# Turning and storing the last quarter of the output by TensorE, in a fused attention and feed-forward kernel

## The chip, the core and the metric

The kernel runs on one core of a Trainium2 chip. The metric is the device time of one execution in microseconds (us). The kernel before took 904.01 us, the median of three runs (902.47 to 904.57). A separate execution was recorded by the hardware profiler; all profile times below are from it, counted from the start of its span. In the profile PE is TensorE (matmuls; PEld its weight loads), DVE is VectorE, ACT is ScalarE, POOL is GpSimd and SP is SyncE, which only issues transfers. A "q" after a name (SPq, ACTq) means the engine's instruction queue.

## The reference

Attention with a mask by cluster: every query and key is assigned to the nearest of 16 centroids of its head, and a query sees only keys of its own cluster. Its output, laid out as 3072 tokens by 512 features, goes through two matrix products with a gate between them. All is float32.

```python
mask = q_assign[:, :, :, None] == k_assign[:, :, None, :]
scores = np.where(mask, scale * np.matmul(q, k.transpose(0, 1, 3, 2)), -1e9)
attn = softmax(scores)                              # over the keys
x = np.matmul(attn, v).transpose(0, 2, 1, 3).reshape(B * S, H * D)   # 4*768, 8*64
h = x @ w_in                                        # 512 -> 2048
g = h * (1.0 / (1.0 + np.exp(-1.702 * h)))
return (g @ w_out).astype(np.float32)               # 2048 -> 512, the output
```

The inputs arrive as 64-bit floats. The kernel reads them as pairs of 32-bit words and makes float32 weights of them itself, which it calls rounding.

## The kernel before, in words

The kernel has a fast path, `fast`, and behind it a `general` one. `fast` returns a number `bad`; a branch at L34 jumps over `general` when it is 0, as it is here. Every engine takes this branch when it has come to the end of its own part of `fast`.

`fast` has two stages. In the first, until about 343 us, attention is computed for 16 pairs of heads in 96 steps of a hand-written order (L665 to L708). In two of the six steps of a pair, `step()` is called five times; each call lets `rounding()` issue its next VectorE instruction. A piece of weights is 128 partitions by 512 columns; pieces 0 to 15 are `w_in`, pieces 16 to 31 are `w_out`. A piece takes five VectorE instructions, and the last of them, at L207, adds two parts and writes the float32 weights. For `w_out` it writes the columns in another order: column 128*r + 32*n + t of the matrix goes to place 128*n + 32*r + t.

In the second stage the tokens of one batch entry (768) pass through both products before those of the next. Each product is done by a scheme with seven multiplications in place of eight for a matrix cut into two by two, and the second product (`second49`) cuts each of the seven once more. The output of a batch entry is gathered in four tiles, `Y[11]`, `Y[12]`, `Y[21]` and `Y[22]`: the first digit is the half of the output columns, the second the half of the tokens. Each has the output columns on the partitions (128 by 2, the second called `m`) and 384 tokens on the free axis. In the last call of `second49` (k = 6, i = 4) the sums that complete `Y[21]` are made by VectorE at L928, L929 and L933. The last one adds the last product to the tokens of `q` = 0 (192 tokens, the first half of the tile) with `m` = 1.

Because the tiles have columns on the partitions, they are turned before they are stored. `store` does it with VectorE's transpose, which turns blocks of 32 by 32 each in its place (L957). After it, a partition holds, for a token, 32 columns of `m` = 0 and 32 of `m` = 1; with the order of `w_out`'s columns these are 64 neighbouring columns of the output, 256 bytes. Four transfers, one for each group of 32 partitions, store a tile or a part of it (L961). The tiles `E` and `T_of` hold the turned data.

For the last batch entry, `Y[22]` is turned and stored within the last call of `second49`. Within it too, before the last product (`extra(2)`, the generator `tail`), `q` = 1 of `Y[21]` is turned and stored by four transfers on SP, and `m` = 0 of `q` = 0 is turned. After the call, `m` = 1 of `q` = 0 is turned, and `q` = 0 is stored by four transfers, alternately on SP and on ScalarE's queue (L1066).

The order of the instructions on an engine is that of the program text, and each engine waits by counters for what it needs from another. Each transfer, too, counts up one of eight counters when it has landed. The counters are given out by the framework, not in the text.

Of the kernel before, what the change touches and what calls it, by code (L numbers as in the profile page):

```python
# [8 lines left out]
FP32 = mybir.dt.float32  # L9
# [5 lines left out]
ALU = mybir.AluOpType  # L15
# [23 lines left out]
def fast(  # L39
# [26 lines left out]
    nc = tc.nc  # L66

    B, H, S, D = q.shape
    NC = centroids.shape[1]
    DM, DF = moe_w_in.shape  # L70
    P = 128
# [12 lines left out]
    SQ = 32  # L84
# [10 lines left out]
        name="spill", bufs=1, space=bass.MemoryType.DRAM))  # L95
# [13 lines left out]
        name="dram", bufs=2, space=bass.MemoryType.DRAM))  # L109
# [3 lines left out]
    def bank():  # L113
        return ps_m.tile([P, 512], FP32, name="m")
# [42 lines left out]
    WN = 512  # L157
# [6 lines left out]
    NW = len(w_chunks)  # L164
    w_raw, w_pow = {}, {}

    def load_w(i):
        if i < NW:
            t = wp.tile([P, WN, 2], I32, name="raw")
            nc.sync.dma_start(out=t.rearrange("p n t -> p (n t)"),  # L170
                              in_=w_chunks[i][1])
            w_raw[i] = t
# [7 lines left out]
    def rounding():  # L180


        i = w_done[0]
        load_w(i + 2)
        raw, w = w_raw.pop(i), w_chunks[i][0]
        e = wp.tile([P, WN], I32, name="e", bufs=2)
        a = bank()
        hi, lo, a_i = raw[:, :, 1], raw.bitcast(U32)[:, :, 0], a.bitcast(I32)
        nc.vector.tensor_scalar(out=a_i, in0=hi, scalar1=3, scalar2=0x3FFFFFF8,
                                op0=ALU.logical_shift_left,  # L190
                                op1=ALU.bitwise_and)
        yield
        nc.vector.scalar_tensor_tensor(out=a_i, in0=hi, scalar=ODD, in1=a_i,
                                       op0=ALU.bitwise_and, op1=ALU.bitwise_or)
        yield
        nc.vector.tensor_scalar(out=e, in0=a_i, scalar1=POWER, scalar2=None,
                                op0=ALU.bitwise_and)
        yield
        e = e.bitcast(FP32)
        nc.vector.scalar_tensor_tensor(out=e, in0=lo, scalar=2.0 ** -52, in1=e,  # L200
                                       op0=ALU.mult, op1=ALU.mult)
        yield
        if i >= NW // 2:
            w, a, e = (w.rearrange("p (n r t) -> p r n t", r=P // SQ, t=SQ),
                       *(x.rearrange("p (r n t) -> p r n t", r=P // SQ, t=SQ)
                         for x in (a, e)))
        nc.vector.tensor_tensor(out=w, in0=a, in1=e, op=ALU.add)  # L207

        check_w(i, raw, raw.bitcast(FP32)[:, :, 1])
        w_done[0] += 1  # L210
        yield
# [13 lines left out]
    def check_w(i, raw, z):  # L225

        tests.append(lambda: nc.scalar.activation(  # L230
            out=z, in_=raw.bitcast(FP32)[:, :, 1], func=AF.Square,
            accum_out=row_sums[:, 2, i:i + 1]))
        tests.append(lambda: nc.scalar.activation(
            out=z, in_=z, func=AF.Exp, scale=-2.0 ** 12,
            bias=fifteen[:, 0:1], accum_out=row_sums[:, 3, i:i + 1]))
# [7 lines left out]
    ident = const.tile([P, P], FP32, name="ident")  # L243
# [46 lines left out]
    def keep_busy(n):  # L290
        for _ in range(n):
# [8 lines left out]
                        identity=ident)  # L300
    for a in range(2):
        rows = slice(a * D, (a + 1) * D)
        nc.vector.tensor_copy(
            out=cT[rows, :, a, :],
            in_=cps[rows, 0:P].rearrange("d (h a c) -> d h a c", a=2,
                                         c=NC)[:, :, a, :])
# [290 lines left out]
    T_of = {}  # L597
# [44 lines left out]
    for p in range(1, NPAIR):  # L642
        for i in range(2 if p == 1 else 0, len(PREP)):
            t = 2 * TG * (p - 1) + (0, 0, 0, 0, 1, 2, 2)[i]
# [65 lines left out]
    while tests:  # L710
# [14 lines left out]
    QT = HALF // 2  # L725
# [4 lines left out]
    ps_b = ctx.enter_context(tc.tile_pool(name="ps_b", bufs=6, space=PS))  # L730
    G = sp.tile([P, NF, 2, HALF], FP32, name="G")
    Z_of = {i: sp.tile([P, FB, DN], FP32, name=f"Z{i}") for i in (1, 2, 4)}
    Y = {n: acc_p.tile([P, 2, HALF], FP32, name=f"Y{n}")
         for n in (11, 12, 21, 22)}
# [31 lines left out]
    def turn_w(i):  # L766
        a = W_of(i)
        sums(nc.vector, ((a(0, 1), a(0, 0), "-", a(0, 1)),))
# [110 lines left out]
    def after7(f):  # L879

        sums(nc.vector, ((G[:, f, 1], G[:, f + FB, 1], "-", G[:, f, 1]),))
        if f >= FQ:
            for _ in sums_t(0, slice(f - FQ, f - FQ + 1)):
                pass

    def second49(k, extra, last):
# [45 lines left out]
        if i == 4:  # L932
# [9 lines left out]
                    5: ((Y[12], y, "+", Y[12]), (Y[22], y, "+", Y[21])),  # L942
                    7: ((Y[22], y, "+", Y[22]), (Y[21], y, "+", Y[21]))}[i])

    def store(b, n, m=slice(0, 2), q=slice(0, 2), queues=(nc.sync,),
              turned=slice(0, 2)):

        h, t = divmod(n, 10)
        h, t = h - 1, t - 1
        o = {11: T_of[4], 12: E[0], 22: E[1], 21: E[2]} if b < B - 1 else {  # L950
            11: T_of[4], 12: T_of[4], 22: T_of[2], 21: T_of[3]}
        o = o[n].rearrange("p a t -> p (a t)").rearrange(
            "p (j m i) -> p j m i", m=2, i=SQ)
        at, to = q.start * QT, q.stop * QT
        o = o[:, at // SQ:to // SQ]
        for one in range(turned.start, turned.stop):
            nc.vector.transpose(out=o[:, :, one], in_=Y[n][:, one, at:to])  # L957
        rows = out[b * S + t * HALF + at:b * S + t * HALF + to]
        for r in range(P // SQ if queues else 0):
            col = r * P + (2 * h + m.start) * SQ  # L960
            queues[r % len(queues)].dma_start(  # L961
                out=rows[:, col:col + (m.stop - m.start) * SQ].rearrange(
                    "(j t) i -> t j i", t=SQ),
                in_=o[r * SQ:(r + 1) * SQ, :, m].rearrange(
                    "t j m i -> t j (m i)"))
# [20 lines left out]
    def do(steps, n):  # L986
        for _ in range(n):
            next(steps, None)
# [3 lines left out]
    for b in range(B):  # L992
        for f in range(FB):
            first7(b, f, *XT)
            sums_w(b * FB + f + 2)
            if f:
                after7(f - 1)
            do(pend, 1)
            if b == 0 and f < 3:
                for n in range(3 * f, min(3 * f + 3, FB)):  # L1000
                    sums_z((nc.gpsimd, nc.vector, nc.vector)[n % 3], n)
            if b == 0 and f in (3, 4):
                for i in ORDER[0:4] if f == 3 else ORDER[4:]:
                    turn_w(i)
            if b == 0 and f >= 3:
                for k in {3: (0,), 4: (1, 2), 5: (3,), 6: (4,), 7: ()}[f]:
                    keep_w(k, spare_y())
                if 5 <= f < 7:
                    load_sums(f - 5)
        after7(FB - 1)  # L1010
        if b < B - 1:
            for h in range(2):
                for hp in range(HP):
                    x = xT_of[b + 1, h, hp] = xp.tile([P, HALF], FP32,
                                                      name="x")
                    nc.sync.dma_start(out=x, in_=kept[b, h, hp])
            made = sums_x(b + 1)
        else:
            made = iter(())

        def stores(b, *todo, **how):
            for n in todo:
                store(b, n, **how)
                yield

        def tail():
            store(b, 22)
            yield
            store(b, 21, q=slice(1, 2))
            store(b, 21, q=slice(0, 1), queues=(), turned=slice(0, 1))  # L1030
            yield

        def chain(*todo):
            for steps in todo:
                yield from steps

        def sums_of_x():
            for XT[:] in made:
                yield

        x_steps = sums_of_x()
        final = b == B - 1

        for k in range(7):
            nxt = sums_t(k + 1) if k < 6 else iter(())
            more = {1: sums_G(6), 2: sums_G(5), 3: sums_G(4),
                    4: stores(b, 11), 5: stores(b, 12) if final else x_steps,
                    6: tail() if final else x_steps}.get(k, iter(()))
            if b == B - 1 and k < 2:
                test(k)  # L1050
            if (b, k) == (B - 1, 6):
                is_bad = nc.values_load(bad[0:1, 0:1], min_val=0, max_val=1)

            def extra(at):
                do(nxt, (2, 1, 1)[at])
                do(more, ((1, 0, 1) if final else (0, 4, 4))[at] if k == 6
                   else (0, 0, 4)[at] if k == 2 else (0, 2, 2)[at])

            second49(k, extra, final)
            if k < 5:  # L1060
                load_sums(k + 2, b == 0 and k > 2)
            elif b < B - 1:
                load_sums(k - 5)
        pend = () if final else stores(b, 12, 22, 21)
        if final:
            store(b, 21, q=slice(0, 1), turned=slice(1, 2),  # L1066
                  queues=(nc.sync, nc.scalar))
    return is_bad
@with_exitstack
def general(  # L1070
# [436 lines left out]
```

## Time and profile before

| | |
|---|---|
| median of three runs | 904.01 us |
| the profiled execution's own time | 905.66 us |
| its span in the profile | 903.8 us |
| TensorE busy | 885.9 us |
| VectorE busy | 728.1 us |
| end of the last matmul | 892.2 us |
| mean granted TensorE clock | 0.995 |

The span is from the first to the last instruction of the program. The profiled execution's own time is 1.9 us longer than its span. A row of the profile names line, engine, operation, what is written and read, shapes and count. The timeline gives start, duration, engine and line, and joins neighbours of one kind. The list of waits says which instruction waited for which, for how long in total, how often, and the longest.

### The profile page before, as it was taken

How to read it: one execution, taken by the hardware profiler on the slowest of the kernel's cores; microseconds unless marked ns; L12 is line 12 of the kernel's file. 1: busy time of each engine (PE TensorE's matmuls, PEld its weight loads, DVE VectorE, ACT ScalarE, POOL GpSimd, SP SyncE). 2: the span in 40 equal slices, each digit the busy share in tenths (PEclk: the TensorE clock that was granted, in tenths of full speed). 3: DMA queues.
4: the chain of work that ended last, by engine and by line, in shares of the span. 5: the costliest groups of instructions: out<-in, count | busy, mean ns of one | idle time of the engine just before them, and what ended most of it. 6: DMA issues, size and time to landing. Idle time of an engine off the chain costs nothing.

```text
span 903.8 us, 17747 instructions
## 1 busy us (share of the span) xinstructions
PE 885.9 (98%) x6712; PEld 581.7 (64%) x6712; DVE 728.1 (81%) x1170; ACT 365.0 (40%) x816; POOL 499.2 (55%) x469
## 2 busy tenths in 40 slices
PE   8999999999999999999999999999999999999994
PEld 3444444444454445558996557997557997557994
DVE  3999989999898997998998557797556797556894
ACT  3677767776777764222111222112222112222110
POOL 5899999999999998693274211242221242220230
PEclk9999999999999999999999999999999999999998
DMA  9466556666664210036213102332102322200323
GB/s 181 113 123 116 103 119 134 139 140 137 138 134 112 85 43 18 9 127 214 70 54 122 36 1 71 105 86 83 42 1 70 106 74 90 47 1 1 105 73 71
DMA packets 177565, 78.97 MB, mean 87 GB/s; under 512 B 154440, under 2 KB 160704, under 8 KB 177472
## 3 DMA queue, kind: packets, MB, share of 16 engines
q1 hardware_dynamic: 176912, 77.63, 35.3%
q8 instruction: 55, 0.90, 0.4%
q14 instruction: 38, 0.31, 0.1%
q10 hardware_dynamic: 560, 0.13, 0.1%
HBM read 61.03 MB, written 16.70 MB: 86 GB/s over the span
## 4 chain that ended last, share of the span: by engine, by line
PE 88%; DVE 6%; issue 2%; POOL 2%; DMA 1%; SPq 0%; ACT 0%; DVEq 0%; POOLq 0%
PE b L850 32%; PE b L900 23%; PE s L468 13%; PE o L533 12%; PE m L550 3%; PE s L491 3%; DVE G L594 2%; POOL sum L517 2%; DVE E L594 1%; PE m L344 1%; DVE Tx L594 1%; DMA in<-in_k_dram 1%; DVE y L841 0%; PE o L292 0%; DMA Wz<-kept_w 0%
## 5 line engine op out<-in xcount | busy, mean ns | idle before, releaser
L517 POOL TENSOR_TENSOR sum<-sum,A 128x384 f32<-128x384 f32 x252 | 265.9, 1091 | 26.7 <-ACT A L499 16.0
L841 DVE TENSOR_TENSOR G<-b,G 128x384 f32<-128x384 f32 x224 | 123.2, 557 | 98.9 <-PE b L850 89.3
L499 ACT ACTIVATE A<-s 128x768 f32<-128x768 f32 x192 | 146.2, 808 | 91.8 <-PE s L491 73.0
L594 POOL TENSOR_TENSOR Y<-y,Y 128x768 f32<-128x768 f32 x28 | 69.2, 2487 | 174.9 <-DVE y L841 151.0
L855 ACT ACTIVATE G<-G 128x384 f32<-128x384 f32 x128 | 66.4, 523 | 199.0 <-DVE G L841 197.7
L468 PE MATMUL s<-T,T 64*64 64x384 f32 x1536 | 143.0, 487 | 0.7 <-ACT A L499 0.7
L533 PE MATMUL o<-A,inv 64*64 64x384 f32 x1536 | 141.4, 483 | 0.0
L594 POOL TENSOR_TENSOR W<-w_in 128x256 f32<-128x256 f32 x32 | 23.6, 738 | 163.8 <-PE b L850 163.5
L594 DVE TENSOR_TENSOR G<-G 128x768 f32<-128x768 f32 (+1 forms) x92 | 102.3, 1136 | 0.0
L468 PEld LDWEIGHTS s<-T,T 64*64 64x64 f32 x1536 | 55.2, 132 | 69.9 <-ACT A L499 36.4
L850 PE MATMUL b<-Tx,w_in 128*128 128x384 f32 x256 | 93.0, 486 | 0.0
L850 PE MATMUL b<-x,W 128*128 128x384 f32 x256 | 93.0, 486 | 0.0
L850 PE MATMUL b<-x,w_in 128*128 128x384 f32 x256 | 88.6, 486 | 0.0
L533 PEld LDWEIGHTS o<-A,inv 64*64 64x64 f32 x1536 | 59.1, 133 | 37.9 <-issue 32.8
L850 PEld LDWEIGHTS b<-x,W 128*128 128x128 f32 x256 | 48.6, 190 | 33.9
L850 PEld LDWEIGHTS b<-Tx,w_in 128*128 128x128 f32 x256 | 48.6, 190 | 33.9
L850 PEld LDWEIGHTS b<-x,w_in 128*128 128x128 f32 x256 | 48.5, 190 | 33.5 <-issue 0.6
L900 PE MATMUL b<-G,w_out 128*128 128x192 f32 x320 | 55.9, 326 | 0.0
L900 PEld LDWEIGHTS b<-G,w_out 128*128 128x128 f32 x320 | 52.7, 190 | 1.1
L900 PE MATMUL b<-E,Wz 128*128 128x192 f32 x288 | 51.5, 328 | 1.4 <-DVE E L594 1.4
L900 PEld LDWEIGHTS b<-E,Wz 128*128 128x128 f32 x288 | 47.1, 190 | 3.4 <-POOL Wz L594 1.3
L850 PE MATMUL b<-Tx,W 128*128 128x384 f32 x128 | 46.6, 487 | 1.5 <-DVE Tx L594 1.5
(165 smaller groups left out, 1366.9 us busy)
## 6 DMA issues: line engine op xcount, KB each, us to landing
Wz<-kept_w SPq DMA_DIRECT2D x78, 256.0 KB
raw<-in_moe_w_in_dram SPq DMA_DIRECT2D x16, 512.0 KB
raw<-in_moe_w_out_dram SPq DMA_DIRECT2D x16, 512.0 KB
inv<-in_v_dram SPq DMA_DIRECT2D x16, 384.0 KB
in<-in_q_dram SPq DMA_DIRECT2D x60, 96.0 KB
in<-in_k_dram SPq DMA_DIRECT2D x60, 96.0 KB
kept<-x SPq DMA_DIRECT2D x24, 192.0 KB
x<-kept SPq DMA_DIRECT2D x24, 192.0 KB
```

The source lines that it names most:

```text
L344: nc.tensor.matmul(out=ps[r:r + SQ, w * NJ * SQ:(w + 1) * NJ * SQ] .rearrange("p (j t) -> p j t", t=SQ), lhsT=cT[:, p % HP].rearrange("p a ...
L468: nc.tensor.matmul(out=ps[c:c + D, a, 0:HALF], lhsT=T[p, 1][rows, kt * P + c:kt * P + c + D], rhs=T[p, 0][rows, h * HALF:(h + 1) * HALF], ...
L491: nc.tensor.matmul(out=s_of[u][c:c + D, a, :], lhsT=rows_of[1, p % 2][rows, kt * P + c:kt * P + c + D], rhs=rows_of[0, p % 2][rows, h * HA ...
L499: nc.scalar.activation(out=A_of[u], in_=s_of.pop(u), func=AF.Exp, scale=SCALE)
L517: nc.gpsimd.tensor_tensor(out=sum_of[g][:, a], in0=(A_of[u - 1] if kt == 1 else sum_of[g])[:, a], in1=A_of[u][:, a], op=ALU.add)
L533: nc.tensor.matmul(out=o_of[g][a * D:(a + 1) * D, r, 0:HALF], lhsT=v_in[p][rows, a, kt, :], rhs=A[rows, a, :], start=(kt == 0), stop=(kt = ...
L550: nc.tensor.matmul(out=ps[a * D:(a + 1) * D, 0:HALF], lhsT=twos, rhs=sm[:, a, :], start=(i == 0), stop=(i == len(parts) - 1))
L594: engine.tensor_tensor(out=o, in0=a, in1=b, op=(ALU.add if op == "+" else ALU.subtract))
L841: nc.vector.tensor_tensor(out=o, in0=p, in1=a, op=ALU.add)
L850: nc.tensor.matmul(out=ps[:, 0:HALF], lhsT=a[:, c], rhs=x(c), start=(c == 0), stop=(c == 1))
L855: nc.scalar.activation(out=g, in_=g, func=AF.Gelu_apprx_sigmoid, scale=2.0)
L900: nc.tensor.matmul(out=ps, lhsT=A[n][:, f], rhs=M[n][:, f], start=start and f == 0, stop=(f == FQ - 1), skip_group_check=True)
```

## The change

In `rounding`, the last addition of a piece of `w_out` is done in two halves of 256 columns, and in another order of the columns: within each half, column 64*r + 32*m + t goes to place 128*m + 32*r + t. What a block-wise transpose leaves beside each other is now part of one run of 256 columns, so in `store` the first column of a transfer changes and nothing else.

A new function `store_last` turns and stores all of `Y[21]` of the last batch entry. It is called after the last `second49`, in place of the last `store`; the steps of `tail` that turned and stored parts of `Y[21]` are gone. It takes `q` = 1 first, then `q` = 0. For each it makes four transposes on TensorE of 128 partitions by 96 tokens, into one bank of PSUM for `q` = 1 and two for `q` = 0. A copy puts each 96 tokens by 256 columns into SBUF: for `q` = 1 two copies on ScalarE, for `q` = 0 one on VectorE and one on ScalarE. A token's 256 columns are one piece of 1 KB in the output. They are stored by one transfer on SP for `q` = 1, and by one on SP and one on ScalarE's queue for `q` = 0.

```diff
-        if i >= NW // 2:
-            w, a, e = (w.rearrange("p (n r t) -> p r n t", r=P // SQ, t=SQ),
-                       *(x.rearrange("p (r n t) -> p r n t", r=P // SQ, t=SQ)
-                         for x in (a, e)))
-        nc.vector.tensor_tensor(out=w, in0=a, in1=e, op=ALU.add)
+        if i < NW // 2:
+            nc.vector.tensor_tensor(out=w, in0=a, in1=e, op=ALU.add)
+        else:
+            for c in (slice(0, WN // 2), slice(WN // 2, WN)):
+                nc.vector.tensor_tensor(
+                    out=w[:, c].rearrange("p (m r t) -> p r m t", m=2, t=SQ),
+                    in0=a[:, c].rearrange("p (r m t) -> p r m t", m=2, t=SQ),
+                    in1=e[:, c].rearrange("p (r m t) -> p r m t", m=2, t=SQ),
+                    op=ALU.add)
...
+    def store_last(b):
+        n = QT // 2
+        for q in (1, 0):
+            o = T_of[3 + (q == 0)].rearrange("p a t -> p (a t)")[
+                0:n, 0:4 * P].rearrange("p (k r m i) -> p k m r i", k=2, m=2,
+                                        i=SQ)
+            pss = [ps_b.tile([P, 512], FP32, name="b") for _ in range(2 - q)]
+            banks = [ps[0:n].rearrange("p (k m r i) -> p k m r i", k=2, m=2,
+                                       i=SQ) for ps in pss]
+            for m in range(2):
+                for k in range(2):
+                    at = q * QT + k * n
+                    nc.tensor.transpose(
+                        out=banks[k % len(banks)][:, k, m].rearrange(
+                            "p r i -> p (r i)"),
+                        in_=Y[21][:, m, at:at + n], identity=ident)
+            for k, queue in ((slice(0, 2), nc.sync),) if q else (
+                    (slice(0, 1), nc.sync), (slice(1, 2), nc.scalar)):
+                ps = banks[k.start % len(banks)]
+                if q or k.start:
+                    for one in range(k.start, k.stop):
+                        nc.scalar.copy(o[:, one], ps[:, one])
+                else:
+                    nc.vector.tensor_copy(out=o[:, 0], in_=ps[:, 0])
+                at = b * S + q * QT + k.start * n
+                queue.dma_start(
+                    out=out[at:at + (k.stop - k.start) * n, 2 * P:4 * P]
+                    .rearrange("(k p) i -> p k i", p=n),
+                    in_=o[:, k].rearrange("p k m r i -> p k r m i")
+                    .rearrange("p k r m i -> p k (r m i)"))
...
-            col = r * P + (2 * h + m.start) * SQ
+            col = (h * P + r * SQ) * 2 + m.start * SQ
...
             store(b, 22)
             yield
-            store(b, 21, q=slice(1, 2))
-            store(b, 21, q=slice(0, 1), queues=(), turned=slice(0, 1))
-            yield
...
         if final:
-            store(b, 21, q=slice(0, 1), turned=slice(1, 2),
-                  queues=(nc.sync, nc.scalar))
+            store_last(b)
```

## The prediction

> **What bounds the kernel now.** I read the busy shares first, then the chain of work that ended last, then the timeline and the queue waits of the last 20 us, because the change touches the tail and one step of the rounding.
>
> The page, span, busy times and chain:
>
> ```profile
> span 903.8 us, 17747 instructions
> PE 885.9 (98%) x6712; PEld 581.7 (64%) x6712; DVE 728.1 (81%) x1170; ACT 365.0 (40%) x816; POOL 499.2 (55%) x469
> PE 88%; DVE 6%; issue 2%; POOL 2%; DMA 1%; SPq 0%; ACT 0%; DVEq 0%; POOLq 0%
> ```
>
> TensorE paces the body: it is idle for 18 us in all, and more than 11 of them are the end. The chain that ended last stops at 893.6 (a VectorE transpose), although the span is 903.8. The last 10 us belong to queues, which the chain does not follow. So the timeline of the end (start, us, engine, line, operation):
>
> ```profile
> 891.74 0.49 PE L900 MATMUL b<-E,w_out 128*128 128x192 f32 x2
> 891.83 0.35 DVE L841 TENSOR_TENSOR Y<-y,Y 128x192 f32<-128x192 f32 x1
> 892.10 0.89 DVE L957 STREAM_TRANSPOSE Tx<-Y 128x192 f32<-128x192 f32 x3
> 892.76 0.80 SPq L961 DMA_DIRECT2D out_dram<-Tx  x2
> 892.91 0.32 DVE L841 TENSOR_TENSOR Y<-b,Y 128x192 f32<-128x192 f32 x1
> 893.26 0.38 DVE L957 STREAM_TRANSPOSE Tx<-Y 128x192 f32<-128x192 f32 x1
> ...
> 893.67 0.85 ACTq L961 DMA_DIRECT2D out_dram<-Tx  x2
> 897.03 2.09 SPq L961 DMA_DIRECT2D out_dram<-Tx  x4
> ```
>
> SP issues two of the six stores left to it, stops at 893.56, and goes on only at 897.03. ScalarE's queue, meanwhile, issues its two at once. SP's own waits in the same stretch (waited for: total, times, longest):
>
> ```profile
> SPq L961 <- DVE Tx L957: 3.5, 1, 3.5
> SPq L961 <- DMA out_dram<-Tx: 3.5, 1, 3.5
> SPq L34 <- SPq L34: 2.6, 1, 2.6
> ```
>
> The first row is honest waiting for the turned data (889.4 to 892.8). The second is the hole: 3.5 us for another store to land. In the program as built, each transfer counts up one of eight completion counters, and a queue may issue a transfer only when the one before it on the same counter has landed. SP's third store of the second half (q = 1) has the counter of ScalarE's first store, which comes earlier in the order of counters but is issued at 893.67, after SP's second. So SP waits for it to land. The trace's record of that counter has 14 of its 16 counts by 895.38, one at 895.93 and the last at 897.02; SP goes on at 897.03.
>
> The third row is SP's jump at L34, over the general kernel that is not needed: from 899.18 to 901.84, 2.66 us. By then the last store had already landed (last count 900.42). From 901.84 to the span's end at 903.78 it is another 1.94 us of closing waits. So the end is: last issue by SP, plus 0.06, plus 2.66, plus 1.94.
>
> **What the Trainium skill says.** "DMA: Bandwidth & Descriptors", section "Why a DMA increments its semaphore by 16 and not by 1": each DMA engine adds one when its share has landed, and only all 16 mean landed. The trace agrees (the counter above), and shows that one late share is enough. "Runtime: NRT & Kernel Launch", section "Instruction fetch mechanics": a taken branch to code outside the fetched window waits for a DMA fetch. The trace agrees: 2.66 us on SP, 2.70 on ScalarE (894.61 to 897.31), 3.10 on VectorE, and instruction packets of 8 and 16 KB lie in between. "TensorE: Matmul & The Clock Gate", section "Part 4: PE-mode transpose": the result lands in PSUM and needs a copy, and it takes some 275 ns in a kernel. The transposes at L370 took 273 ns, 110 ns apart.
>
> **The change, part by part.**
>
> *Rounding.* For 16 pieces of w_out, the add of 128x512 at L207 (691 ns, both for w_in written straight and for w_out written in its order) becomes two of 128x256. No equal row exists. "VectorE: DVE Perf Modes", section on the TRN2 errata, prices a float32 add at (N+151)/0.96 ns: 691 at 512, which the trace has exactly, and so 424 at 256. That is 2 x 424 - 691 = 157 ns a piece, 2.5 us in all. From below it is about 16 x 60 ns = 1 us, since neighbouring VectorE instructions here overlap by some 80 ns. All lie between 175 and 340 us. There VectorE was busy 152.9 of 165 us and TensorE 164.9: 12.1 us of slack on VectorE, 0.76 us a piece. At 340.2 VectorE waits 2.8 us for TensorE's sums, so a small lag is caught up before the next stage. Queued behind the new add are the next rounding step and normalise; who waits for these is a step or more away. I cost it at 0; without cover it is 1.0 to 2.5 us.
>
> *Other stores.* Same 256-byte pieces, only other columns: 0.
>
> *VectorE's end.* Three transposes go from in front of the last add, and one from behind it. The add then waits for the add before it (to 892.18) and for the last matmul (to 892.23): 892.27 to 892.59, where it was 892.91 to 893.23. Gain 0.64.
>
> *TensorE's end.* Eight transposes of 128x96 are queued behind the last product, at 110 ns. The third waits for the add that ends at 892.18, so the fourth starts at about 892.34 and ends at 892.61. The fifth and sixth fit in before the last add ends. The seventh starts at 892.64, the eighth at 892.75 and ends at 893.02.
>
> *Copies.* A ScalarE copy out of PSUM took 319 ns for 128x192 and 479 for 128x384, so 372 for 256 columns. The first waits for the fourth transpose: 892.66 to 893.03; the second to 893.43; the third (first quarter-half, k = 1) to 893.84. VectorE copies the other eighth: 416 ns between its rows of 192 and 384 from PSUM, after the seventh transpose, 892.96 to 893.38.
>
> *Stores.* Eight issues become three. SP's issue of the store with q = 1 has moved behind the last product and both copies: 893.47 to 893.9, where its first had gone at 892.76. SP's second follows at 893.94 to 894.4; ScalarE's at 893.9 to 894.3. An issue took 0.31 to 0.70 us. As built, these three count on counters whose last transfers have long landed (the latest by 886.5), and none on ScalarE's. The 3.5 us wait has no successor; nothing of the program stands behind it.
>
> *The end.* SP jumps at 894.45, is back at 897.1, and must then find the three stores landed. A store took 1.7 us from issue to its last count (898.68 to 900.42) when nothing disturbed it, and 3.35 us (893.67 to 897.02) when instruction packets lay on one of its engines. The jumps of PE, VectorE, ScalarE and SP now fall close together with the stores, so I take the dear value for the last: 893.94 + 3.35 = 897.3. With 1.94 us the span is 899.24, against 903.78: 4.5 us less. The profiled execution took 905.66 for a span of 903.78; the median of the runs is 904.01. I take the same difference from the median: 899.5.
>
> **The rivals.**
>
> *Fetches and stores collide more.* Four jumps and three stores within 1.5 us: a store's last share, or SP's own code, comes later still. The late share was worth 1.64 us (895.38 to 897.02). Once more on top of my dear value gives 901.1. For it: the 16-KB packet at 894.7 took 1.19 us. Against: only 384 pieces of 1 KB instead of 1536, and the body is over.
>
> *Nothing is won.* The wait is replaced by another, such as a copy or store that waits for an older counter, or the jump of an engine that ends later now (PE's took 3.65 us, from 893 it would be back at 896.7, under SP's 897.1). For a time of 903 to 904 something must hold SP until 901; no wait of the built program does.
>
> *Slower.* The two adds for 16 pieces, between 175 and 340 us, cost more than the price, because each writes runs of 32 elements. Up to 0.76 us a piece it is hidden; slower than before needs (12.1 + 4.5)/16 = 1.04 us a piece, so a half of 0.87 us instead of 0.42. At 1.4 us a half (the dearest VectorE rows of such kind, 1429 ns for 768 elements) it is 2.1 us a piece, 34 us in all, less 16.6: 921. Against: L207 took 691 ns with these runs and without.
>
> **How the numbers follow.** As worked out: 0.66, 898.5 to 900.6. More collision: 0.21, 900.6 to 902.2. Nothing won: 0.07. Slower: 0.06. The predicted time is the first's, 899.5. The range goes from 898.5 (undisturbed stores and fetches: SP back at 896.6) to 902.0 and leaves out the last two and the edges. About 0.2% (1.8 us) is what a measurement of this kernel can tell: faster 0.87, same 0.07, slower 0.06.
>
> **What would show it.** SP's wait for a store disappears and its last issue ends near 894.4; its jump begins there. The eight transposes stand 110 ns apart, the last ending near 893.0; the copies take some 370 to 420 ns. The adds of the rounding take about 424 ns and TensorE reaches the first matmul of L850 at 342.9 as before. I am wrong if that moment moves by a microsecond or more, if SP waits at the end for anything other than its jump and the landings, or if a store of 1-KB pieces takes more than 3.5 us to land.

## The result, and the profile after

The kernel after took 900.34 us (median of seven runs, 898.76 to 901.91). The kernel before, run beside it, took 904.57 us (seven runs, 902.47 to 905.15). The ratio is 0.9957, with a 95% interval from 0.9947 to 0.9967: 4.2 us less by the medians, 3.9 by the ratio. The forecast was 4.5 us less.

The profiled execution took 900.34 us itself, for a span of 898.5. The page's span, busy times and chain of the kernel after:

```profile
span 898.5 us, 17781 instructions
PE 885.8 (99%) x6720; PEld 581.4 (65%) x6720; DVE 728.3 (81%) x1183; ACT 366.1 (41%) x819; POOL 497.4 (55%) x469
PE 87%; DVE 8%; issue 2%; POOL 1%; DMA 1%; ACT 0%; SPq 0%; DVEq 0%; ACTq 0%; POOLq 0%
```

The busy times are those of before within 2 us; TensorE's is 885.8 for 885.9. So the gain is not less work but less idle time of TensorE. The chain again does not follow the queues at the end. The two spans differ by 5.2 us, more than the medians do. Part of that is the body: the last product ends at 891.30, not at 892.23. That is no more than this moment varies from one execution to another: in the experiments that keep the rounding and all the work of before it lies between 889.07 and 891.21. I therefore compare tails: the time from the end of the last product's last matmul to the end of the span. It was 903.78 - 892.23 = 11.55 us and is now 898.54 - 891.30 = 7.24 us, 4.31 us less. "Plus x" below means x us after the end of the last product.

The timeline of the end, kernel after (start, us, engine, line, operation; neighbours of one kind are joined):

```profile
890.82 0.49 PE L904 MATMUL b<-E,w_out 128*128 128x192 f32 x2
...
891.14 1.04 PE L962 MATMUL b<-ident,Y 128*96 128x128 f32 x8
891.34 0.36 DVE L845 TENSOR_TENSOR Y<-b,Y 128x192 f32<-128x192 f32 x1
891.78 0.91 ACT L971 COPY Tx<-b 96x256 f32<-96x256 f32 x3 [2.72 <-PE b L962]
892.11 0.42 DVE L973 COPY Tx<-b 96x256 f32<-96x256 f32 x1 [0.41 <-PE b L962]
892.44 1.55 SPq L975 DMA_DIRECT2D out_dram<-Tx  x2
892.72 0.36 ACTq L975 DMA_DIRECT2D out_dram<-Tx  x1
```

The eight transposes (the L962 row), the last add, the four copies and the three stores stand in the order that was worked out. One row is longer than forecast: SP's two issues take 1.55 us together. The second of them alone, in a narrower stretch:

```profile
892.86 1.13 SPq L975 DMA_DIRECT2D out_dram<-Tx  x1
```

SP's own waits of the kernel after, from 870 us on (waited for: total, times, longest):

```profile
SPq L975 <- ACT Tx L971: 3.8, 1, 3.8
SPq L34 <- SPq L34: 2.5, 1, 2.5
```

The first is the wait for the turned data. The wait of 3.5 us for another store has no row any more. The second is SP's jump, from plus 2.78 to plus 5.30 in the trace. The three stores' last counts come at plus 3.73, 3.96 and 4.51, inside the jump, so the landings cost nothing; 5.30 + 1.94 us of closing waits is the tail of 7.24.

The rounding's additions of the kernel after (form: min/median/max ns, first and last start), and then VectorE's share of the stretch in which they lie, kernel after and kernel before (busy us and number of instructions of each engine, clock, DMA share):

```profile
L207 DVE TENSOR_TENSOR w_out<-m,e x32: 411/418/425, 179.6 to 334.9; 128x256 f32<-128x256 f32 x32
```

```profile
175.00:340.00 165.00, 165.00 (x2152) 77.22 (x2143) 152.80 (x266) 120.08 (x265) 156.81 (x146) 1.00 0.50 114
```

```profile
175.00:340.00 165.00, 164.92 (x2148) 78.32 (x2144) 152.88 (x251) 118.91 (x263) 156.28 (x147) 1.00 0.50 113
```

Sixteen more instructions in all, 15 of them by the count of this stretch, and 418 ns for each half; yet TensorE has no idle time in the stretch (165.00 of 165). The additions take 16 x (2 x 418 - 691) = 2.3 us more, and VectorE's busy time is still not higher: what else falls into the stretch varies by about as much (151.7 us in a second profile of the kernel after).

### The profile page after: what moved, and what is told of

It is laid out like the page before. It is cut to its first block, busy times and chain, and to the rows that moved or that the text cites. A ratio compares the mean times of both kernels' runs of the same rounds, so it can differ in the third digit from the quotient of the medians.

```text
span 898.5 us, 17781 instructions
## 1 busy us (share of the span) xinstructions
PE 885.8 (99%) x6720; PEld 581.4 (65%) x6720; DVE 728.3 (81%) x1183; ACT 366.1 (41%) x819; POOL 497.4 (55%) x469
## 4 chain that ended last, share of the span: by engine, by line
PE 87%; DVE 8%; issue 2%; POOL 1%; DMA 1%; ACT 0%; SPq 0%; DVEq 0%; ACTq 0%; POOLq 0%
PE b L854 32%; PE b L904 23%; PE s L472 13%; PE o L537 12%; PE s L495 3%; PE m L554 3%; DVE G L598 2%; DVE E L598 2%; POOL sum L521 1%; PE m L348 1%; DVE Tx L598 1%; DMA in<-in_k_dram 1%; DVE x L598 0%; DVE e L200 0%; DVE y L845 0%
## 5 line engine op out<-in xcount | busy, mean ns | idle before, releaser
L598 POOL TENSOR_TENSOR Y<-y,Y 128x768 f32<-128x768 f32 x28 | 67.4, 2421 | 175.0 <-DVE y L845 151.0
L598 DVE TENSOR_TENSOR G<-G 128x768 f32<-128x768 f32 (+1 forms) x92 | 104.5, 1159 | 0.0
```

Source lines behind the costliest of these rows:

```text
L598: engine.tensor_tensor(out=o, in0=a, in1=b, op=(ALU.add if op == "+" else ALU.subtract))
```

## The experiments

The theory: SP's stop of 3.5 us went because no store counts behind a late one any more, and the end follows SP's jump. The rivals: the gain is the earlier sums, the larger pieces or the smaller number of transfers, and the stop would be replaced by something else if it alone were removed. All ratios are to the kernel before on the same chip, with 95% intervals.

### The rounding alone

The kernel before with the new order of the columns of `w_out` and nothing of the new end.

```diff
-        if i >= NW // 2:
...
-        nc.vector.tensor_tensor(out=w, in0=a, in1=e, op=ALU.add)
+        if i < NW // 2:
+            nc.vector.tensor_tensor(out=w, in0=a, in1=e, op=ALU.add)
+        else:
+            for c in (slice(0, WN // 2), slice(WN // 2, WN)):
+                nc.vector.tensor_tensor(
+                    out=w[:, c].rearrange("p (m r t) -> p r m t", m=2, t=SQ),
...
-            col = r * P + (2 * h + m.start) * SQ
+            col = (h * P + r * SQ) * 2 + m.start * SQ
```

> The kernel before with only the new column order of w_out: the rounding's last add in two halves, and the stores' first columns to match. Theory (hidden): the 32 adds take about 418 ns each, VectorE's waiting between 175 and 340 us shrinks from 12.1 us to about 10, the first product of the second stage starts where it did (within 0.5 us of 342.9), and the time is that of the kernel before, within 0.1%. Rival (the rounding is on the path): 1.0 to 2.5 us longer, 905.6 to 907. The end is unchanged in both: SP still stands still for about 3.5 us.

904.27 us against 904.01, ratio 1.0003 (0.9995 to 1.0010); the tail is 11.67 us, and SP's stop is there as before:

```profile
SPq L965 <- DMA out_dram<-Tx: 3.5, 1, 3.5
```

The rounding costs nothing that can be measured, so the whole gain lies in the end. It also shows how little the start of the second stage says: its first matmul is at 341.4 here, at 342.9 in the kernel before, and at 339.7 and 341.9 in the next two kernels, which have the rounding of before.

### The stop alone

Three kernels keep everything of before and only send the last eight stores to other queues. In the first, ScalarE's two go to GpSimd's queue, in the second all go to SP, in the third all four of `q` = 0 go to ScalarE. The three lines with a plus are those of the three kernels in turn.

```diff
             store(b, 21, q=slice(0, 1), turned=slice(1, 2),
-                  queues=(nc.sync, nc.scalar))
+                  queues=(nc.sync, nc.gpsimd))
+                  queues=(nc.sync,))
+                  queues=(nc.scalar,))
```

> The kernel before, with the two last stores that ScalarE's queue had given to GpSimd's queue, whose transfers count on counters of their own; VectorE's transposes and the 256-byte pieces stay. Theory (the shared counter): SP issues its six stores without a stop, from about 0.5 us after the last matmul's end in steps of some 0.47 us, so its last issue ends about 3.4 us after the last matmul instead of 6.9, and the span shrinks by 2.5 to 3.6 us, the lower figure if GpSimd's own stores land late. Rival (pieces or transposes are what cost): nothing or less than 0.7 us is gained, SP still stops.

> The kernel before, with all eight stores of the last quarter on SP. Theory (the shared counter): no stop of SP, but two more issues; the last issue ends about 4.3 us after the last matmul's end instead of 6.9, the time is 2.2 to 2.8 us shorter. Rival (a queue full of small pieces stops SP, whichever counter it waits for): SP stops as before or longer, no gain.

> The kernel before, with all four stores of q = 0 on ScalarE's queue and only the four of q = 1 on SP. As built, SP's first store of q = 1 now counts on the counter of ScalarE's first. Theory (the shared counter): though SP has two issues fewer, it stops before its first store until ScalarE's first has landed, some 3 us after its issue, and issues all four after it: the last issue ends 6 to 7 us after the last matmul, the time is within 1 us of the kernel before. Rival (number of issues on SP, or pieces): two issues fewer on SP, the time is 1 to 3 us shorter.

| | time, us | ratio | tail, us |
|---|---|---|---|
| GpSimd's queue | 901.36 | 0.9977 (0.9966 to 0.9989) | 9.40 |
| all on SP | 903.43 | 0.9995 (0.9987 to 1.0004) | 10.43 |
| four on ScalarE | 904.29 | 1.0003 (0.9995 to 1.0012) | 10.61 |

The third keeps the wait, and moves it. SP's waits in it:

```profile
SPq L961 <- DMA out_dram<-Tx: 6.9, 1, 6.9
```

ScalarE's first store has its 16th count at plus 4.07, and SP's first store is issued at plus 4.13. SP's whole queue is held by the landing of a store on another queue. (The profiled execution of this kernel, at 901.94 us, is faster than its median; its tail stands for that one execution.)

The first two lose the wait, as expected, but gain less than was forecast for it: 2.1 and 0.5 us by the ratios, of the expected 2.5 to 3.6 and 2.2 to 2.8. The first interval (1.0 to 3.1 us) reaches into what was expected, and the second (up to 1.2 us) does not exclude that nothing was gained, so it is the trace that says where the rest is. SP's waits when all is on SP, followed by its fifth issue in that kernel:

```profile
SPq L961 <- DVE y L841: 15.5, 2, 11.7
SPq L961 <- DVE Tx L957: 4.7, 2, 3.5
SPq L34 <- SPq L34: 2.7, 1, 2.7
```

```profile
893.82 1.58 SPq L961 DMA_DIRECT2D out_dram<-Tx  x1
```

No wait is listed, and yet one issue takes 1.58 us where the two before it and the three behind it take 0.43 to 0.47. What goes on during it, by the view of the transfers (queue, kind: packets, MB, share of 16 engines; 893.6 to 895.1):

```profile
q1 hardware_dynamic: 423, 0.10, 33.0%
q8 instruction: 1, 0.02, 5.4%
q14 instruction: 1, 0.01, 1.3%
```

One instruction packet of 16 KB is under way: 5.4% of 16 engines for 1.5 us is 1.3 us on one engine. In the trace it lasts from plus 2.50 to plus 3.78, and the issue ends at plus 4.18, 0.40 later. With GpSimd's queue the same: an issue of 1.70 us, ended at plus 4.25, packet ended at plus 3.84. In the kernel before, that packet (2.48 to 3.67) fell into SP's stop, where it held nothing up. The stop had hidden it.

For all on SP the sum closes. The stop is gone (-3.48). The eight issues take 4.79 us in place of the six's 2.66 (+2.13). The gaps between them add about 0.15. The last issue ends 1.21 us earlier (plus 5.69 for plus 6.90) and the tail is 1.12 shorter, as the jump took 0.1 longer. With GpSimd's queue the six issues take 3.93 us: -3.48 + 1.27 = -2.21, and the last issue ends 2.16 earlier.

### The packet moved

If the packet belongs to TensorE's jump at L34, it should come later when TensorE ends later. One transpose that nobody reads is put on TensorE behind the last product, once in the kernel before and once with all stores on SP.

```diff
+            ps = ps_b.tile([P, 512], FP32, name="b")
+            nc.tensor.transpose(out=ps[0:QT // 2, 0:P],
+                                in_=Y[21][:, 1, QT:QT + QT // 2],
+                                identity=ident)
             store(b, 21, q=slice(0, 1), turned=slice(1, 2),
```

> The kernel before plus one TensorE transpose that nothing reads, behind the last product; it waits for VectorE's sum that ends as the last product does. Its only use is that TensorE comes to its jump about 2.2 us later. Theory (fetches of TensorE's jump hold up a share of the stores): its two 16-KB instruction packets move from about 1.2 before and 2.5 after the last product's end to about 1 and 4 after it; ScalarE's first store lands near 3.2 instead of 4.8, SP's stop shortens from 3.5 to about 2 us, and the time is 1.0 to 1.8 us shorter, with all eight stores and VectorE's transposes as before. Rival (the late share has another cause, such as the stores' own number): no change, within 0.5 us.

> All eight stores of the last quarter on SP, and the unread late transpose on TensorE. Theory (two causes, the shared counter and the fetch): neither SP's stop nor the long fifth issue of 1.6 us is left, SP issues every 0.47 us and ends 4.3 to 4.6 us after the last product; from the last product's end to the span's end it is about 9.1 us, and the time is 2.0 to 2.6 us shorter than before. Rival (the fifth issue is long because four stores of small pieces are under way): it stays at about 1.6 us, and the end is that of all stores on SP without the transpose, 10.4 us, within 0.3.

904.25 us (0.9999, 0.9990 to 1.0008) and 903.91 us (0.9995, 0.9986 to 1.0004). SP's stop did shrink in the first, to 1.1 us, but nothing was gained, and the reason is in the stores of the first (engine, operation, count: min/median/max ns):

```profile
L961 SPq DMA_DIRECT2D out_dram<-Tx x7: 315/442/1834, 888.0 to 897.3; - x7
L961 ACTq DMA_DIRECT2D out_dram<-Tx x2: 355/618/880, 892.4 to 892.8; - x2
```

TensorE's two packets did move, from -1.24 and plus 2.48 to plus 0.93 and plus 4.51. The hold moved with them, to SP's second issue (1.83 us, ending at plus 2.72, packet ended at 2.32), to ScalarE's second (also ending at 2.72), and to SP's fifth (ending at 6.36, packet ended at 5.91). With all on SP the fifth issue is short again (0.39 us), and the second and the seventh are held instead. The expected 1.0 to 1.8 us, and 2.0 to 2.6 with all on SP, were not to be had: I had forecast where the two packets would go, but not which issues would then lie under them. That the hold follows the packet is thereby shown, and not only seen side by side.

### Without the jump

In the next two, the branch and `general` are left out, of the kernel before and of the kernel after.

```diff
-    with tc.If(bad > 0):
-        general(tc, *args)
```

> The kernel before without the general path, which is not taken with these inputs: no branch stands behind the fast path. Theory (SP's jump sets the end once its stores are issued, and the jumps' fetches hold up stores): no jump of 2.6 us; SP's stop is shorter too; the end follows the last landing, about 1.3 us after SP's last issue. The time is 2.0 to 4.0 us shorter. Rival (landing of the last store sets the end): less than 0.7 us.

> The changed kernel without the general path, which is not taken with these inputs. Theory (the jump sets the end): SP needs no jump, the last of the three stores lands about 1.8 us after its issue at the latest (4.5 us after the last product's end in the changed kernel), so the end is some 0.8 to 1.5 us earlier than in the changed kernel, 4.8 to 5.7 us shorter than the kernel before. Rival (landing sets the end): as the changed kernel, 4.0 to 4.4 us shorter than before.

The kernel before so: 900.45 us (0.9949, 0.9933 to 0.9966), tail 7.11; that is 4.6 us less by the ratio, 3.8 by the medians, and 2.0 to 4.0 were expected. The kernel after so: 897.81 us (0.9922, 0.9905 to 0.9939), tail 5.26. SP's waits at the end of the first:

```profile
SPq L959 <- DMA out_dram<-Tx: 1.9, 2, 1.8
SPq L1500 <- DMA out_dram<-Tx: 0.9, 2, 0.5
```

The stop is still there, but 1.8 us long in place of 3.5: the counter is full at plus 3.11, SP goes on at plus 3.13. So the counter made the wait, and the instruction packets of the jumps made almost half of its length. At L1500 SP now waits for the landings; without the jump the end follows these.

The stores of the second, and the transfers from 893.3 to 894.6 in it:

```profile
L973 SPq DMA_DIRECT2D out_dram<-Tx x2: 318/356/393, 893.3 to 893.7; - x2
L973 ACTq DMA_DIRECT2D out_dram<-Tx x1: 362/362/362, 893.6 to 893.6; - x1
```

```profile
q1 hardware_dynamic: 97, 0.10, 30.1%
```

No instruction packet, and SP's second issue takes 0.39 us, not 1.13. The last landing is at plus 3.83 in place of 4.51. The expected gain over the kernel after was 0.8 to 1.5 us; it was 2.0 by the tails (by what each is under before, 2.2 by the medians and 3.2 by the ratios). The tail's 2.0 is the 0.79 by which the jump outlasted the landing, 0.68 of earlier landing, and 0.51 of shorter closing waits (1.43 after the landing, not 1.94 after the jump). The last two were not reckoned with.

### Pieces of 256 bytes

The kernel after, with the column order of before: the same transposes and copies, but 256-byte pieces again, and a transfer for each 96 tokens, so four in all.

```diff
-                queue.dma_start(
-                    out=out[at:at + (k.stop - k.start) * n, 2 * P:4 * P]
...
+                for one in range(k.start, k.stop):
+                    at = b * S + q * QT + one * n
+                    queue.dma_start(
+                        out=out[at:at + n, :].rearrange(
+                            "p (r x) -> p r x", r=4)[:, :, P // 2:P],
...
```

> The changed kernel with the old order of w_out's columns: TensorE turns the last quarter and the copies are the same, but a token's 256 columns go out as four pieces of 256 bytes, and the store of q = 1 is cut in two, so four transfers instead of three. Theory (the number of issues and what stops them sets the end, not the pieces): from the last product's end to the span's end 7.2 us plus at most one issue, 7.3 to 7.9; 3.6 to 4.3 us shorter than the kernel before. Rival (1-KB pieces are what brings it): more than 8.5 us from the last product to the end, less than 3 us shorter than before.

901.2 us (0.9970, 0.9959 to 0.9981), tail 8.21. The tail lies between what the two theories gave. The time, 2.7 us less than before (1.7 to 3.7), is on the rival's side, though its interval reaches into both. SP's three issues take 0.72, 1.17 and 0.57 us; the last ends at plus 3.52 in place of 2.69, and this 0.83 is most of the tail's 0.97. By the tail, three quarters of the gain come without the larger pieces; by the ratios, two thirds. (The profiled execution, 899.95 us, is again faster than the median.) The rest is the fourth transfer and longer issues: ScalarE's took 0.72 us for 384 pieces of 256 bytes and 0.36 for 96 of 1 KB.

### Two versions that avoid the held issue

An issue was held only where another one on its queue was just before it. ScalarE's single issue in the kernel after began 0.04 us after the packet and took 0.36 us. So one version gives each queue one store: all of `q` = 1 on ScalarE's, all of `q` = 0 on SP's. Another lets TensorE end later, with an unread transpose that waits for ScalarE's last copy.

```diff
+        for q, queue in ((1, nc.scalar), (0, nc.sync)):
+            at = b * S + q * QT
+            queue.dma_start(
+                out=out[at:at + QT, 2 * P:4 * P]
+                .rearrange("(k p) i -> p k i", p=n),
...
```

```diff
             store_last(b)
+            ps = ps_b.tile([P, 512], FP32, name="b")
+            nc.tensor.transpose(
+                out=ps[0:P, 0:QT // 2],
+                in_=T_of[4].rearrange("p a t -> p (a t)")[0:QT // 2, 2 * P:3 * P],
+                identity=ident[0:QT // 2, 0:QT // 2])
```

> The changed kernel with two stores instead of three: q = 1 on ScalarE's queue, all of q = 0 on SP, each after its copies; turns and copies as they were. Theory (a second issue on a queue cannot finish before the instruction packet on a DMA engine has, some 2.3 us after the last product's end; a first one can): SP's only store is issued from about 1.45 to 1.8 us after the last product's end, against 2.69 for SP's second; SP jumps 0.9 us earlier, and the end is 6.3 to 6.7 us after the last product instead of 7.24; the time is 0.5 to 0.9 us shorter than that of the changed kernel. Rival (the long issue belongs to the size of what is under way): SP's store of 192 KB takes a microsecond or more to issue, no gain.

> The changed kernel plus one unread TensorE transpose that waits for ScalarE's last copy, so that TensorE jumps about 1 us later. Theory (the fetch of TensorE's jump makes SP's second issue long): the 16-KB packet moves from 1.4 to about 2.4 us after the last product's end, SP's second issue takes 0.3 to 0.5 us instead of 1.13 and ends near 1.95; the end is 6.4 to 6.9 us after the last product, unless a store's late share (which may now land up to 4.6) or TensorE's own return holds it. Rival (the second issue is long for another reason): it stays at about 1.1 us and the end at 7.2.

> The changed kernel itself, on the same chip as the three others, for comparison: 3.7 to 4.7 us shorter than the kernel before, the end about 7.2 us after the last product's end, SP's second issue about 1.1 us.

| | time, us | ratio | tail | SP's last issue | SP's jump | back at |
|---|---|---|---|---|---|---|
| one store on each queue | 899.72 | 0.9955 (0.9941 to 0.9968) | 7.29 | 0.32 us | 3.5 us | plus 5.36 |
| TensorE later | 900.05 | 0.9956 (0.9942 to 0.9969) | 7.31 | 0.40 us | 3.25 us | plus 5.29 |
| the kernel after again | 900.23 | 0.9955 (0.9942 to 0.9969) | 7.87 | 1.80 us | 2.5 us | plus 5.93 |

SP's waits in the version with one store on each queue:

```profile
SPq L34 <- SPq L34: 3.5, 1, 3.5
```

Both versions do what they were made for: SP's last issue ends at plus 1.73 and 1.95, not 2.69. Neither gains. The jump begins earlier and takes longer, and SP is back where it was. In the second version a shorter jump would have brought nothing either: the last count of SP's second store came at plus 5.54, and SP, back at 5.29, waited 0.1 us for it. The kernel after again shows how much the packet varies from one execution to the next; SP's second issue in it is

```profile
891.53 1.80 SPq L975 DMA_DIRECT2D out_dram<-Tx  x1
```

with a packet from plus 1.39 to plus 3.02. I have no version that keeps `general` and is measurably faster than the kernel after: the three intervals lie on each other. Why the jump takes 3.25 to 3.5 us when it begins within 0.3 us of ScalarE's was not tested. That the fetches of several engines hold each other up is a guess.

## Why the prediction was right, point by point

**SP's stop.** Right in place, cause and disappearance: no wait for a store is left, and in five kernels, with stops of very different lengths, SP's store is issued 0.02 to 0.06 us after the last count of ScalarE's first store (plus 4.79 in the kernel before, 4.86 with the rounding alone, 4.07 with four on ScalarE, 3.78 with TensorE later, 3.11 without the jump). But "nothing of the program stands behind it" was only half the question. Behind it stood the instruction packet that it had covered. Taken away alone, the stop was worth 2.1 us with GpSimd's queue, and 0.5 us, not told from nothing, with all on SP; not 3.5. The change reaches 4.2 because it also takes away issues. From the start of SP's first issue behind the last product to the end of its last it was 6.37 us and is 1.55: 3.48 for the stop, 1.21 for issues (2.66 for six, 1.45 for two), 0.13 for gaps. Of these 4.82 us, 0.61 is given back, since SP's first issue comes at plus 1.14 and not at plus 0.53. That leaves 4.21 of the 4.31 by which the tail is shorter; 0.1 is the jump.

**The rounding.** Right. An add of half a piece took 418 ns against the 424 worked out from the Trainium skill ("VectorE: DVE Perf Modes", section on the TRN2 errata), and the experiment with it alone shows no cost. The sign that I named for it was poor, though. TensorE's first matmul of the second stage moved by 0.94 us, just under the microsecond that I had set as the bound. Kernels without the new rounding move by more (339.7 and 341.9 for 342.9). Two sums of the forecast are off by little: with the overlap of 80 ns that it names, its lower cost is 16 x 77 ns = 1.2 us, not 1; and the lower edge of its range, 898.5, is the span for SP back at 896.6, which as a time would be 898.8.

**VectorE's, TensorE's and the copies' end.** Right within 0.1 us, but for ScalarE's third copy. The last add ends at plus 0.39 (0.36 predicted). The transposes are 110 ns apart and the last ends at plus 0.87 (0.79). ScalarE's copies end at 0.84, 1.11 and 1.39 (0.80, 1.20, 1.61), closer together than worked out, since each starts 0.10 us before the one ahead of it ends. VectorE's ends at 1.22 (1.15).

**The stores.** The first two were issued a little early, at plus 1.14 and 1.42 (1.24 and 1.67). SP's second was the term that failed: 1.13 us in place of 0.46, and 1.80 in the repetition. Its 0.46 is the price of an issue with no packet over it. The dearest issue of the range it gives, 0.70 us, is one with a packet over it: SP's fifth in the kernel before, followed here by the instruction packet among the transfers of 897.8 to 898.7.

```profile
897.94 0.70 SPq L961 DMA_DIRECT2D out_dram<-Tx  x1
```

```profile
q14 instruction: 1, 0.01, 4.2%
```

The packet, 8 KB, lasts from plus 5.68 to 6.29, and the issue ends at 6.42. The trace before thus already showed an issue that was held, and the forecast took it for scatter.

**The end.** I let the last landing decide, at the dear 3.35 us, plus 5.07. It was at 4.51, 2.96 us from issue, and decided nothing. The jump did: it began at 2.74 (2.22 predicted), took 2.56 (2.66) and ended at 5.30 (4.88). Two errors cancel, since the landing was sized 0.56 too dear and the issue 0.67 too cheap. That the forecast tail, 7.01, is so close to 7.24 and 7.87 is therefore luck.

**The rivals.** "Fetches and stores collide more" named the right collision, but in the landing; it took place in the issue. It cost 0.7 us, and 1.4 in the repetition, against the 0.39 us of that issue without a packet, and the median stayed with the first case. "Nothing is won" and "slower" did not come about.

## What to carry to other kernels

Before a stall is counted as a gain, list what else goes on during it, instruction fetches included: what it covered becomes the next stall, as with 3.5 us of stop that were worth 2.1 or less alone. At the end of a kernel fewer transfers can be worth more than the mere sum of their issue times, since each one issued right behind another may be held; from three to two, though, nothing was gained here. When an end is followed by a jump, look whether the jump's end moves with its start before work is spent on starting it earlier.

## What was unexpected of the hardware

An issue can be held by an instruction fetch, and no list of waits shows it. While a 16-KB instruction packet was under way, an issue on SP's or ScalarE's queue right behind another one on its queue ended 0.29 to 0.50 us after the packet's end. That is so for every such issue at the end of these kernels that began under the packet, or at most 0.05 us before it:

| kernel | packet ends | issue ends | issue takes, us |
|---|---|---|---|
| all on SP | 3.78 | 4.18 | 1.58 |
| GpSimd's queue | 3.84 | 4.25 | 1.70 |
| four on ScalarE | 3.01 | 3.30 | 0.96 |
| before with TensorE later, SP's and ScalarE's second | 2.32 | 2.72, 2.72 | 1.83, 0.88 |
| the same, SP's fifth | 5.91 | 6.36 | 1.50 |
| the same with all on SP | 2.20, 5.69 | 2.59, 6.08 | 1.70, 1.47 |
| 256-byte pieces | 2.36 | 2.86 | 1.17 |
| after | 2.27 | 2.69 | 1.13 |
| after again | 3.02 | 3.36 | 1.80 |

Three issues that had begun 0.11 to 0.37 us before the packet were not held: ScalarE's second with the rounding alone and with four on ScalarE (0.45 us each), and SP's sixth with TensorE later and all on SP (0.46). Nor was GpSimd's second in the kernel with its queue: 0.57 us from plus 2.46, under a packet from 2.48 to 3.84. Without any packet over it the second issue on a queue took 0.39 to 0.45 us. A packet of 8 KB held an issue too, in five cases: these took 0.58 to 0.79 us and ended 0.13 to 0.27 us after the packet. An issue that did not follow right behind another was not held: 0.32 us on SP with one store on each queue, from plus 1.41 to 1.73, under a packet from 1.39 to 2.54. The Trainium skill ("DMA: Bandwidth & Descriptors", section "Queues, rings and completion order") says that each DMA engine serves its queues in turn and finishes a whole packet of one before it goes on to the next; by a packet it means a group of descriptors, where the profile counts single records. That fits a 16-KB packet which keeps one of sixteen engines for 0.9 to 1.6 us, and the last shares that came 1.6 us behind the fourteenth in the kernel before. No run here shows the turns themselves, nor how such a packet holds the issuing queue.
